# A fused attention and mixture-of-experts kernel: one written list of pieces with named PSUM banks, and means of values put into later blocks by transfers

## The chip, the cores and the metric

The kernel runs on one core of a Trainium2 chip. The metric is the device time of one execution in microseconds (us). One execution of the kernel before was also profiled.

## What is computed

The reference, cut to what matters. `q`, `k`, `v` have the shape (4, 8, 768, 64): batches, heads, positions, head size.

```python
k_sum = k.reshape(B, H, nb, 32, D).max(axis=3)       # nb = 24 blocks of 32 positions
v_sum = v.reshape(B, H, nb, 32, D).mean(axis=3)
scores_l = where(|pos_q - pos_k| < 16, scale * q @ k^T, -1e9)
scores_s = scale * q @ k_sum^T + log(32)
a = softmax(concatenate([scores_l, scores_s]))
x = a @ concatenate([v, v_sum])                      # then (3072 tokens, 512)
e = argmax(x @ w_gate)                               # one of 8 experts for each token
out = softmax(x @ w_gate)[e] * sigmoid(x @ w_output_gate)[e] * (relu(x @ w1[e]) @ w2[e])
```

## The kernel before

Attention goes over 24 tiles of 128 tokens, six to a batch, numbered 0 to 23. A tile is two blocks of 64 queries. A block's keys stand in `kt` (88 columns to a block) and its values in `vw`: 96 rows of neighbouring positions, with rows 64 to 87 kept for the 24 means of the whole batch. One product of a block with `vw` therefore takes in the local window and the summaries. Two copies of `kt` and `vw` alternate by batch.

The steps, with the functions of the code and the tile names that rows of the profile show:

- `load` and `load_vw` (L257) bring `raw_k`, `raw_q` and `vw` from DRAM, mostly from SyncE's queue (SP). `reorder` copies them into `nat_k` and `nat_q` (L246). `prep_k` and `prep_q` transpose them on TensorE (PE) into `ktr` and `qtr` (L291); ACT copies these into `kt` and `qt` (L221), and DVE takes the maximum of keys by block (`km`, L305). `k_sum` spreads it over `kt` (L312).
- `means` (L264, L267) sums values into the bank `ms`; `gather_means` makes `mg` (L273), which ACT copies to `mst`, 24 rows. `put_means` copies `mst` into rows 64 to 87 of the two blocks of a tile, one copy on ACT (L221) and one on DVE (L219).
- `scores` fills `sp` (L333) and DVE adds the mask (`pr`, L338); `smallest` (L345), `subtract` on GpSimd (POOL, L350) and `exps` on ACT (L354) follow. `turn_p` transposes `pr` into `pt` (L365) and ACT copies it to `pT`. `values` multiplies with `vw` into `pv` (L376), and `norm` divides (DVE, L386 to L390) into `xs`. `store_x` writes `xs` to `x_dr` (L395).
- `turn_x` (`xtr`, L402), `logits` (`lp`, L411) and `turn_logits` (`lt`, L419) give the logits of two tiles. `route` finds experts and places for a batch: some eight small DVE operations, the counts `rk` and `tot` on PE (L456 to L461), and six scatters of list entries `l_dr` from POOL (L484).

All PSUM banks of attention come from `bank`, which hands the tags `TR`, `S`, `PT`, `PV`, `S`, `PT`, `PV` round in turn, whatever the piece is.

The experts work in slots of 256 tokens. Slots 0 to 2 take tokens of the first two batches alone, so slot 0 can begin while the attention of the last batch runs. `table` computes the slot table in three steps on DVE. `begin` frees the pool of batches 0 and 2, and issues on SP eight loads `w1l` and four `w2l` for slot 0 (L979) and five `raw` loads for slot 1 (L909), 256 KB each. The first of them needs the expert's number from the slot table. `fetch_list` (`lst`, L866) and `fetch` (`xg`, L881) bring the rows of a slot, `take_plain` transposes them (`xp`, L1007), `early_first` is slot 0's first layer (`hp`, L1017), `early_second` its second (`yp`, L1031). `split` turns a `raw` weight of slot 1 into a high and a low part. From slot 1 on `full` does the same with these parts.

The order of all five engines' queues is the order in which the program is written: attention is recorded under a manual schedule. A loop over tiles i records scores of tile i+2, values of tile i-1, turn_p of i and so on, and dictionaries (`todo`, `put`, `mid`, `rts`, `small`, `scat`) hold what is to be recorded with a later tile. The last tiles and slot 0 are written out by hand behind the loop. A queue works in order, so an instruction that waits holds up all that stands behind it on its engine.

Of the kernel before, what the change touches and what calls it, by code (L numbers as in the profile page):

```python
# [56 lines left out]


# [143 lines left out]
def attention(tc, const, sa, sb, st, ps, dr, q, k, v, id_sb, c_sb, wg_sb, x_dr, l_dr, rt, moe, table, begin, swap):  # L202
# [56 lines left out]
    def means(b, m):  # L259
        if m == 0:  # L260
            mps[b] = ps.tile([P, H * D], F32, name=f"ms{b}", tag="MS", bufs=PB["MS"])
        mp = mps[b]
        for j in range(4):
            nc.tensor.matmul(mp[32 * j:32 * j + 32], lhsT=c_sb[0:LW, C_AVG + 32 * m:C_AVG + 32 * m + 32],  # L264
                             rhs=VW[b % 2][0:LW, 4 * m + j, :, 0:D], start=m == 0, stop=m == 2 and j < 3)
# [17 lines left out]
    ms, km, mps = {}, {}, {}  # L283

    def transposed(kind, b, u, g):
        n = nat[kind, b, u]
# [6 lines left out]
        return pt  # L293

    def prep_k(b, u, g):
        kt = KT[b % 2]
        pt = transposed("k", b, u, g)
        if b not in km:
            km[b] = sb.tile([P, HP, NS], F32, name=f"km{b}", tag="km", bufs=2)
        at = PAD + 4 * u * KW  # L300
        src = pt.rearrange("p x (i s) -> p x i s", s=64)
        dst = kt[:, 2 * g:2 * g + 2, at:at + 4 * KW].rearrange("p x (i w) -> p x i w", w=KW)
        evac(dst[:, :, :, 0:48], src[:, :, :, 0:48])
        evac(dst[:, :, :, 48 + NS:KW], src[:, :, :, 48:64])
        nc.vector.tensor_reduce(out=km[b][:, 2 * g:2 * g + 2, 8 * u:8 * u + 8],  # L305
                                in_=pt.rearrange("p x (n s) -> p x n s", s=32), axis=AX.X, op=ALU.max)
# [16 lines left out]
    def scores(i):  # L323
# [4 lines left out]
        for hp in range(HP):  # L328
            for y in range(2):
                blk = 2 * tok + y  # L330
                for x in range(2):
                    r = slice(64 * x, 64 * x + 64)
                    nc.tensor.matmul(sp[x][64 * y:64 * y + 64, hp, 0:W], lhsT=qt[r, hp, P * tt + 64 * y:P * tt + 64 * y + 64],  # L333
                                     rhs=kt[r, hp, blk * KW:blk * KW + W], start=True, stop=True)
        pr = sb.tile([P, 2, HP, W], F32, name=f"pr{b}{tok}", tag="pr", bufs=BUFS["pr"])
# [20 lines left out]
    def turn_p(i):  # L356
        b, tok = tiles[i]
        pr = prs.pop(i)
        e = i < HELD
        pTs[i] = (sa if e else sb).tile([W, 2, HP, P], F32, name=f"pT{b}{tok}", tag="pTe" if e else "pTl",  # L360
                                        bufs=BUFS["pTe" if e else "pTl"])
        for x in range(2):
            pt = bank([W, HP, P], f"pt{b}{tok}{x}")
            for hp in range(HP):
                nc.tensor.transpose(pt[:, hp, :], pr[:, x, hp, :], id_sb)  # L365
            evac(pTs[i][:, x], pt)

    def values(i):
        b, tok = tiles[i]
        pT = pTs.pop(i)  # L370
        pvs[i] = []
        for g in range(2):
            po = bank([P, 4, D + 1], f"pv{b}{tok}{g}")
            for h in range(4 * g, 4 * g + 4):
                for y in range(2):
                    nc.tensor.matmul(po[64 * y:64 * y + 64, h % 4, :], lhsT=pT[:, h % 2, h // 2, 64 * y:64 * y + 64],  # L376
                                     rhs=VW[b % 2][:, 2 * tok + y, h, 0:D + 1], start=True, stop=True)
            pvs[i].append(po)

    def norm(i):  # L380
# [3 lines left out]
        po = pvs.pop(i)  # L384
# [7 lines left out]
    def store_x(i):  # L392
        b, tok = tiles[i]
        n0 = b * S + tok * P
        (nc.sync if i >= 17 else nc.gpsimd).dma_start(x_dr[n0:n0 + P, :], xss[i].rearrange("p h d -> p (h d)"))  # L395

    def turn_x(i):
        b, tok = tiles[i]
        xs = xss[i]
        xp = bank([P, NC, P], f"xtr{b}{tok}")  # L400
        for c in range(NC):
            nc.tensor.transpose(xp[:, c, :], xs[:, 2 * c:2 * c + 2, :].rearrange("p h d -> p (h d)"), id_sb)  # L402
        if tok % 2 == 0:
            xTs[0] = st.tile([P, NC, 2, P], F32, name=f"xT{b}{tok}", tag="xT", bufs=BUFS["xT"])
        evac(xTs[0][:, :, tok % 2, :], xp)

    def logits(b, tok):

        lp = bank([P, 2 * P], f"lp{b}{tok}")
        for c in range(NC):  # L410
            nc.tensor.matmul(lp[32 * c:32 * c + 32, :], lhsT=wg_sb[:, c, :], rhs=xTs[0][:, c].rearrange("p t n -> p (t n)"),  # L411
                             start=True, stop=True)
        xTs[1] = st.tile([P, 2, P], F32, name=f"ls{b}{tok}", tag="ls", bufs=BUFS["ls"])
        evac(xTs[1].rearrange("p t n -> p (t n)"), lp)

    def turn_logits(b, tok):
        lt = bank([P, 2, 2 * E], f"lt{b}{tok}")
        for t in range(2):
            nc.tensor.matmul(lt[:, t, :], lhsT=xTs[1][:, t, :], rhs=c_sb[:, C_SEL:C_SEL + 2 * E], start=True, stop=True)  # L419
# [6 lines left out]
    def route(b):  # L426
# [29 lines left out]
        nc.tensor.matmul(rk[:, 0:TB, :], lhsT=rt["tri"], rhs=ohb, start=True, stop=False)  # L456
        for sft in range(1, TB):
            nc.tensor.matmul(rk[:, sft:TB, :], lhsT=rt["ones"], rhs=ohb[:, 0:TB - sft, :], start=False, stop=sft == TB - 1)
        tot = bank([P, E], f"tot{b}")
        for t in range(TB):  # L460
            nc.tensor.matmul(tot, lhsT=rt["ones"], rhs=ohb[:, t, :], start=t == 0, stop=t == TB - 1)  # L461
# [55 lines left out]
    for tok in range(2, TB):
        load_vw(0, tok, (0,))
    for g in range(2):
        prep_q(*steps[0], g)  # L520
# [709 lines left out]
```

## Time and profile before

| | us |
|---|---|
| three runs | 533.62, 538.9, 537.9 |
| median | 537.9 |
| profiled execution | 536.84 |
| its span | 535.0 |
| mean granted clock of PE | 0.972 |
| PE busy in the span | 491.0 |

Times in the profile count from the span's start. A row of the timeline gives start, duration, engine, line and tile; the bracket at its end is the idle time of that engine before the row, and what ended it. `SPq` rows are the issues of transfers; how long one travels is given as the time to landing.

### The profile page before, as it was taken

What the parts mean: (1) busy time and instruction counts of PE and PEld (TensorE: products, weight loads), DVE (VectorE), ACT (ScalarE), POOL (GpSimd) and SP (SyncE); (2) the same over time, 40 slices, a digit from 0 to 9 for tenths busy, and PEclk for the clock granted to TensorE, in tenths of its full rate; (3) what the DMA queues carried; (4) which work ended last, traced back from release to release, by engine and by line L of the source; (5) the groups of instructions that cost most, each with busy time, mean ns of one, the idle gap of its engine ahead of it and who ended that gap; (6) DMA issues with size and microseconds to landing.
All of it is one profiled execution on the core that took longest, in us unless ns stands there. A gap on an engine that the chain in (4) does not pass through costs nothing.

```text
span 535.0 us, 12519 instructions
## 1 busy us (share of the span) xinstructions
PE 491.0 (92%) x4348; PEld 405.3 (76%) x4348; DVE 355.1 (66%) x787; ACT 313.1 (59%) x612; POOL 232.8 (44%) x261
## 2 busy tenths in 40 slices
PE   7698999998987799999999999999999989989980
PEld 6556577486666686789898998989899869879870
DVE  3748479679876237797657667665756668668672
ACT  4475677576655545464646655554655567566581
POOL 8737535646684606736433240312224315214221
PEclk9899999998997799999999999999999999999996
DMA  9998957865329328996947748484673966967771
GB/s 235 199 236 199 278 129 179 197 154 128 82 56 324 117 92 266 242 168 193 328 141 254 254 168 312 126 310 150 245 260 137 310 212 216 319 210 228 264 238 29
DMA packets 106114, 109.53 MB, mean 205 GB/s; under 512 B 43150, under 2 KB 67886, under 8 KB 106032
## 3 DMA queue, kind: packets, MB, share of 16 engines
q1 hardware_dynamic: 97216, 90.04, 57.6%
q0 software_dynamic: 8816, 18.51, 11.4%
q8 instruction: 38, 0.62, 0.5%
q14 instruction: 44, 0.36, 0.3%
HBM read 98.33 MB, written 13.59 MB: 209 GB/s over the span
## 4 chain that ended last, share of the span: by engine, by line
PE 69%; ACT 9%; DMA 7%; issue 5%; POOL 4%; DVE 4%; SPq 1%; POOLq 0%; ACTq 0%; DVEq 0%
PE yp L1128 8%; PE yp L1127 8%; PE yp L1126 8%; PE hp L950 8%; PE hp L949 8%; PE hp L948 8%; PE pt L365 3%; PE hp L1017 3%; PE yp L1031 3%; PE pv L376 3%; PE sp L333 2%; ACT pr L354 2%; DMA raw<-in_moe_w_dram 2%; PE xp L930 2%; ACT pT L221 2%
## 5 line engine op out<-in xcount | busy, mean ns | idle before, releaser
L918 DVE TENSOR_TENSOR w2l<-raw,w2h 128x512 fp32r<-128x512 f32 x120 | 79.4, 685 | 40.3 <-ACT w2h L917 38.7
L917 ACT ACTIVATE w2h<-raw 128x512 fp32r<-128x512 f32 x120 | 72.9, 628 | 54.8 <-PE yp L1128 23.7
L950 PE MATMUL hp<-xhl,w1l 128*128 128x256 f32 x352 | 99.4, 283 | 0.0
L949 PE MATMUL hp<-xhl,w1h 128*128 128x256 f32 x352 | 99.4, 283 | 0.0
L948 PE MATMUL hp<-xhl,w1h 128*128 128x256 f32 x352 | 99.4, 284 | 0.0
L881 POOL DMA_INDIRECT xg<-x_dr,lst x34 | 39.3, 1155 | 118.1 <-PE xp L930 110.6
L918 DVE TENSOR_TENSOR w1l<-raw,w1h 128x512 fp32r<-128x512 f32 x117 | 74.5, 687 | 14.8 <-ACT w1h L917 13.5
L1126 PE MATMUL yp<-w2h,hh 128*128 128x512 f32 x200 | 80.1, 400 | 0.0
L1128 PE MATMUL yp<-w2h,hl 128*128 128x512 f32 x200 | 78.7, 394 | 0.1
L1127 PE MATMUL yp<-w2l,hh 128*128 128x512 f32 x200 | 78.6, 393 | 0.0
L917 ACT ACTIVATE w1h<-raw 128x512 fp32r<-128x512 f32 x120 | 67.0, 621 | 8.4 <-DMA raw<-in_moe_w_dram 6.9
L949 PEld LDWEIGHTS hp<-xhl,w1h 128*128 128x128 f32 x352 | 67.4, 191 | 1.1 <-issue 0.2
L948 PEld LDWEIGHTS hp<-xhl,w1h 128*128 128x128 f32 x352 | 67.2, 191 | 1.2 <-issue 0.2
L950 PEld LDWEIGHTS hp<-xhl,w1l 128*128 128x128 f32 x352 | 67.4, 192 | 0.0
L951 ACT ACTIVATE hh<-hp 128x256 fp32r<-128x256 f32 x88 | 33.4, 380 | 52.0 <-PE hp L950 50.4
L350 POOL TENSOR_TENSOR pr<-pr,mn 128x960 f32<-128x960 f32 x24 | 43.1, 1797 | 46.1 <-DVE mn L345 29.1
L952 DVE SCALAR_TENSOR_TENSOR hl<-hp,hh 128x256 fp32r<-128x256 f32 x88 | 35.9, 419 | 35.6 <-ACT hh L951 35.5
L1151 POOL DMA_INDIRECT out_dram<-y,lst x27 | 30.5, 1131 | 55.7 <-DVE y L1148 28.9
L221 ACT ACTIVATE pT<-pt 120x512 f32<-120x512 f32 x48 | 26.8, 596 | 41.2 <-PE pt L365 41.0
L338 DVE TENSOR_TENSOR pr<-sp,c_sb 128x480 f32<-128x480 f32 x48 | 29.2, 649 | 29.2 <-PE sp L333 29.2
L866 POOL DMA_INDIRECT lst<-l_dr,rowib x30 | 31.5, 1051 | 31.9 <-issue 21.8
L1128 PEld LDWEIGHTS yp<-w2h,hl 128*128 128x128 f32 x200 | 37.5, 188 | 8.6 <-DVE hl L1097 0.5
(206 smaller groups left out, 876.9 us busy)
## 6 DMA issues: line engine op xcount, KB each, us to landing
raw<-in_moe_w_dram SPq DMA_DIRECT2D x240, 256.0 KB, 5.2
raw_k<-in_k_dram SPq DMA_DIRECT2D x12, 512.0 KB, 6.0
raw_q<-in_q_dram SPq DMA_DIRECT2D x12, 512.0 KB, 6.2
vw<-in_v_dram SPq DMA_DIRECT2D x44, 128.0 KB, 4.9
x_dr<-xs POOLq DMA_DIRECT2D x17, 256.0 KB, 4.0
vw<-in_v_dram SPq DMA_DIRECT2D x33, 64.0 KB, 5.1
w1l<-in_moe_w_dram SPq DMA_DIRECT2D x8, 256.0 KB, 7.9
w2l<-in_moe_w_dram SPq DMA_DIRECT2D x8, 256.0 KB, 5.7
```

The costliest lines, as they stand in the source:

```text
L221: nc.scalar.activation(dst, src, AF.Copy, scale=1.0 if scale is None else scale)
L350: nc.gpsimd.tensor_tensor(pr, pr, mns.pop(i).unsqueeze(2).to_broadcast([P, H, W]), ALU.subtract)
L881: nc.gpsimd.indirect_dma_start(out=self.xg[t], out_offset=None, in_=self.x_dr[0:rows, :], in_offset=bass.IndirectOffsetOnAxis(ap=self.list ...
L917: nc.scalar.activation(hi, raw, AF.Copy)
L918: (lo_by or nc.vector).tensor_tensor(lo, raw, hi.bitcast(F32), ALU.subtract)
L948: nc.tensor.matmul(hp, lhsT=w_h[:, fs], rhs=self.xh[:, c, :], start=c == 0, stop=False)
L949: nc.tensor.matmul(hp, lhsT=w_h[:, fs], rhs=self.xl[:, c, :], start=False, stop=False)
L950: nc.tensor.matmul(hp, lhsT=w_l[:, fs], rhs=self.xh[:, c, :], start=False, stop=c == NC - 1)
L952: nc.vector.scalar_tensor_tensor(hl[:, j, :], hp, 0.0, hh[:, j, :].bitcast(F32), ALU.max, ALU.subtract)
L1126: nc.tensor.matmul(y, lhsT=hh[:, j, tk], rhs=w_h, start=j == 0, stop=False)
L1127: nc.tensor.matmul(y, lhsT=hh[:, j, tk], rhs=w_l, start=False, stop=False)
L1128: nc.tensor.matmul(y, lhsT=hl[:, j, tk], rhs=w_h, start=False, stop=j == NF - 1)
```

## The change

The loop, the dictionaries and the hand-written end are replaced by one string `ORDER` of 895 words, each a piece, read from left to right. A word is a piece's short name, its arguments, and behind a colon the PSUM banks that it takes. Pieces that write a bank and those that copy it out become words of their own (`pk` and `kk`, `mk`; `tp` and `kp`; `sc` and `ma`; `lg` and `kl`). Every yield of `route` and of the slot table is now one operation, so `route` takes 30 words for a batch (`r`) and the table 26 (`ta`).

A put of means is a word for each block, with the engine that does it: 7 words `pu...a` on ACT, 6 `pu...v` on DVE and 35 `pu...s` as a transfer inside SBUF from SP's queue. The puts of batch 0 are all on ACT and DVE. In slot 0 a `split` is a word too (16 of them, 13 on DVE and 3 on POOL). In slot 1 three steps of the later slot table are taken at a time (`REST`), since each is now one operation.

```diff
+ORDER = """
+lk.0 lk.1 lk.2 lq.0 lq.1 lv.0.0.s lv.1.0.s cl.1 rk.0.v pk.0.0:T kk.0.0 cl.0 mk.0.0 pk.0.1:S kk.0.1 mk.0.1 rk.1.a
...
+r.1 ta ta mi.18 r.1 pu.17.0.s r.1 me.3.1 su.18 st.15.p kp.16.0 kp.16.1 lv.23.0.s lv.23.1.s sc.19:SP ma.19 va.16.0:V
...
-    def put_means(b, tok):
-        for blk in (2 * tok, 2 * tok + 1):
-            evac(VW[b % 2][LW:LW + NS, blk, :, 0:D], ms[b][LW:LW + NS], engine="av"[blk % 2])
+    def put_means(t, y, engine):
+        b, tok = tiles[t]
+        blk = 2 * tok + y
+        if engine == "s":
+            nc.sync.dma_start(VW[b % 2][LW:LW + NS, blk, :, 0:D], ms[b][LW:LW + NS])
+        else:
+            evac(VW[b % 2][LW:LW + NS, blk, :, 0:D], ms[b][LW:LW + NS], engine=engine)
...
     def bank(shape, name):
-        tag = next(turn[0])
+        tag = {"S": "S", "P": "PT", "V": "PV", "T": "TR", "M": "MS"}[banks_of.pop(0)]
         return ps.tile(shape, F32, name=name, tag=tag, bufs=PB[tag])
...
-    for i, (b, tok) in enumerate(tiles[:n - AHEAD]):
...
+    for w in ORDER.split():
+        w, _, at = w.partition(":")
+        banks_of[:] = at
+        name, *args = w.split(".")
+        work[name](*(int(x) if x.isdigit() else x for x in args))
+    return [lambda: route_to(B - 1) for _ in range(TB)]
...
-            made = made or next(rest, None)
+            for _ in range(REST):
+                made = made or next(rest, None)
```

Three places show what this does to the queues. The first is SP's queue at the end of slot 0's and slot 1's first weight loads; `vw` from `mst` is a put, `x_dr` a store of a tile's result. Before:

```order
L909 DMA raw_1_3_2526<-in_moe_w_dram 128x512
L909 ISA
L909 DMA raw_1_4_2528<-in_moe_w_dram 128x512
L395 DMA x_dr<-xs_2569 128x512
L395 DMA x_dr<-xs_2667 128x512
L395 DMA x_dr<-xs_2743 128x512
```

And now:

```order
L845 DMA raw_1_3_2544<-in_moe_w_dram 128x512
L845 ISA
L845 DMA raw_1_4_2546<-in_moe_w_dram 128x512
L344 DMA vw_170<-mst_2349 24x8x64 x2
L462 DMA x_dr<-xs_2569 128x512
L344 DMA vw_170<-mst_2349 24x8x64
L462 DMA x_dr<-xs_2672 128x512
L344 DMA vw_170<-mst_2349 24x8x64 x3
```

The puts of tiles 20 to 23 stand behind all 17 weight loads; before, these puts were copies on ACT and DVE.

The second is DVE's queue at the routing of batch 1 (`mx` to `o` are its small operations, `km` a maximum of keys, `mn` a tile's minimum). Before:

```order
L435 TENSOR_REDUCE mx_1934<-lg_1484 128x6
L437 TENSOR_TENSOR d_1936<-lg_1484,mx_1934 128x48
L439 SCALAR_TENSOR_TENSOR fi_1938<-d_1936,c_sb 128x48
L441 TENSOR_REDUCE first_1940<-fi_1938 128x6
L443 TENSOR_TENSOR oh_1942<-c_sb,first_1940 128x48
L445 CAST ohb_1944<-oh_1942 128x48
L447 TENSOR_TENSOR os_1946<-lg_1484,oh_1942 128x48
L449 TENSOR_REDUCE o_1948<-os_1946 128x6
L345 TENSOR_REDUCE mn_1950<-pr_1890 128x8
L305 TENSOR_REDUCE km_1724<-ktr_1956 128x2x8
L305 TENSOR_REDUCE km_1724<-ktr_1964 128x2x8
```

And now:

```order
L508 TENSOR_REDUCE mx_1926<-lg_1482 128x6
L511 TENSOR_TENSOR d_1928<-lg_1482,mx_1926 128x48
L514 SCALAR_TENSOR_TENSOR fi_1930<-d_1928,c_sb 128x48
L517 TENSOR_REDUCE first_1932<-fi_1930 128x6
L370 TENSOR_REDUCE km_1733<-ktr_1906 128x2x8
L520 TENSOR_TENSOR oh_1936<-c_sb,first_1932 128x48
L686 TENSOR_SCALAR ti_early<-ti_early 128x8
L523 CAST ohb_1945<-oh_1936 128x48
L526 TENSOR_TENSOR os_1962<-lg_1482,oh_1936 128x48
L414 TENSOR_REDUCE mn_1964<-pr_1865 128x8
```

The small operations no longer stand in one block ahead of the minimum and the maxima.

The third is POOL's queue at the start (`nat_k` is the third block of keys, the loads are neighbours of later values). Before:

```order
L215 MEMSET vw_170 24x8x64
L246 COPY nat_k_235<-raw_k_182 128x1024
L257 DMA vw_169<-in_v_dram 32x8x64 x11
L257 DMA vw_169<-in_v_dram 16x8x64
L350 TENSOR_TENSOR pr_317<-pr_317,mn_320 128x960
```

And now:

```order
L271 MEMSET vw_169 24x8x64
L313 DMA vw_169<-in_v_dram 32x8x64 x4
L302 COPY nat_k_239<-raw_k_176 128x1024
L313 DMA vw_169<-in_v_dram 32x8x64 x5
L313 DMA vw_169<-in_v_dram 16x8x64
L313 DMA vw_169<-in_v_dram 32x8x64 x2
L419 TENSOR_TENSOR pr_317<-pr_317,mn_320 128x960
```

Four of the loads moved ahead of the copy. The pieces of `ORDER` on PE between the values of tiles 17 and 20 are, in this order: turn_p 18, turn_x 17, scores 21, values 18, turn_p 19, values 19, query transposes with the logits of tiles 16 and 17, turn_x 18, scores 22, turn_p 20 with turn_logits, turn_x 19, scores 23. Behind values 20 come turn_p 21, logits, values 21, turn_x 20, take_plain, turn_p 22 with turn_logits, and slot 0's first layer.

More of the change, by code (lines that the diff above doesn't have):

```diff
@@ L354, in exps, with turn_p, keep_p, values @@
         nc.scalar.activation(pr, pr, AF.Exp, scale=-1.0)
[L356 removed]
+    def turn_p(i, x):
         b, tok = tiles[i]
[L358 to L368, printed above, removed]
[L369 to L378 removed]
+        pt = banks["pt", i, x] = bank([W, HP, P], f"pt{b}{tok}{x}")
+        for hp in range(HP):
+            nc.tensor.transpose(pt[:, hp, :], prs[i][:, x, hp, :], id_sb)
+    def keep_p(i, x):
+        b, tok = tiles[i]
+        if x == 0:
+            e = i < HELD
+            pTs[i] = (sa if e else sb).tile([W, 2, HP, P], F32, name=f"pT{b}{tok}", tag="pTe" if e else "pTl",
+                                            bufs=BUFS["pTe" if e else "pTl"])
+        evac(pTs[i][:, x], banks.pop(("pt", i, x)))
+    def values(i, g):
+        b, tok = tiles[i]
+        po = banks["pv", i, g] = bank([P, 4, D + 1], f"pv{b}{tok}{g}")
+        for h in range(4 * g, 4 * g + 4):
+            for y in range(2):
+                nc.tensor.matmul(po[64 * y:64 * y + 64, h % 4, :], lhsT=pTs[i][:, h % 2, h // 2, 64 * y:64 * y + 64],
+                                 rhs=VW[b % 2][:, 2 * tok + y, h, 0:D + 1], start=True, stop=True)
     def norm(i):
@@ L383, in norm @@
         den = st.tile([P, H], F32, name=f"den{b}{tok}", tag="den", bufs=BUFS["den"])
-        po = pvs.pop(i)
+        po = [banks.pop(("pv", i, g)) for g in range(2)]
         for g in range(2):
@@ L401, in turn_x, with keep_x @@
         for c in range(NC):
-            nc.tensor.transpose(xp[:, c, :], xs[:, 2 * c:2 * c + 2, :].rearrange("p h d -> p (h d)"), id_sb)
+            nc.tensor.transpose(xp[:, c, :], xss[i][:, 2 * c:2 * c + 2, :].rearrange("p h d -> p (h d)"), id_sb)
+    def keep_x(i):
+        b, tok = tiles[i]
         if tok % 2 == 0:
[L404 to L409, printed above, removed]
+            xTs[i // 2] = st.tile([P, NC, 2, P], F32, name=f"xT{b}{tok}", tag="xT", bufs=BUFS["xT"])
+        evac(xTs[i // 2][:, :, tok % 2, :], banks.pop(("xp", i)))
@@ L517, in attention @@
[L517 to L520, printed above, removed]
-    k_sum(0, "v")
-    for u in range(3):
-        load("k", 1, u)
-    n = len(tiles)
-    live, at, held = {}, {}, []
-    for i in range(n):
-        at[i] = []
-        for _ in range(2):
-            if i > HELD and held:
-                live[held[0]] = i
-                at[i].append(held.pop(0))
-        held.append(i)
-    live[n - 1] = n
-    early, todo, put, scat, rts, end, small, mid = {}, {}, {}, {}, {}, {}, {}, {}
@@ L552, in attention @@
-    for t in range(n):
-        first = live[t - t % TB]
-        later(max(live[t] - 2, first - 1), lambda t=t: put_means(*tiles[t]), put)
-    for i in range(AHEAD):
-        scores(i)
-        smallest(i)
-        subtract(i)
-        if i == 0:
-            reorder("q", *steps[1], "a")
-            load("q", *steps[3])
-            for g in range(2):
-                prep_q(*steps[1], g)
-            exps(0)
-    for i in range(3):
-        later(live[2 * TB - 1] + 4 + i, table, small)
-    plan = {
-        live[2 * TB - 1] + 6: [begin],
-        n - AHEAD - 1: [moe.take_plain],
-    }
@@ L633, in attention @@
-    assert not small and not plan and not pools and not scat and not early and not end
-    b = B - 1
-    def first(j, *n):
-        moe.early_first(j)
-        for x in n:
-            moe.split(1, x)
-    t = n - AHEAD
-    values(t - 1)
-    norm(t - 1)
-    turn_p(t)
-    exps(t + 1)
-    for x in put.pop(t):
-        x()
-    for x in mid.pop(t, []) + rts.pop(t, []):
-        x()
-    assert not todo.pop(t, None) and not put and not todo and not rts and not mid
-    store_x(t - 1)
-    first(0, "v", "p")
@@ L1055, in full_with @@
             if not self.slots.get(EARLY):
-                made = made or next(rest)
+                for _ in range(REST):
+                    made = made or next(rest)
                 if made:
```

365 lines of the change are left out of this document (175 added, 190 removed).

## The prediction

> **What bounds the kernel now.** I read the page first, then busy time by stage, then TensorE's timeline with its gaps, then the DMA-issuing queue of SyncE.
>
> ```profile
> PE 491.0 (92%) x4348; PEld 405.3 (76%) x4348; DVE 355.1 (66%) x787; ACT 313.1 (59%) x612; POOL 232.8 (44%) x261
> ...
> PEclk9899999998997799999999999999999999999996
> ```
>
> TensorE (PE) is the bound; its granted clock dips in the 2nd, 10th, 13th and 14th slice, all in the part that the change rewrites. By stage:
>
> ```profile
> 25.00:151.00 126.00, 116.10 (x1733) 79.78 (x1730) 89.86 (x238) 84.39 (x163) 72.13 (x83) 0.99 0.72 170
> 126.00:133.00 7.00, 4.45 (x48) 3.18 (x43) 6.64 (x21) 3.33 (x8) 4.70 (x8) 0.76 0.79 181
> 151.00:170.80 19.80, 15.66 (x226) 13.03 (x222) 15.57 (x39) 9.48 (x16) 13.45 (x15) 0.83 0.68 204
> 151.00:184.30 33.30, 25.27 (x328) 20.70 (x325) 21.24 (x54) 17.22 (x29) 22.86 (x23) 0.79 0.61 191
> 163.00:170.00 7.00, 7.00 (x88) 6.17 (x84) 5.16 (x10) 1.73 (x4) 4.09 (x5) 0.52 1.02 340
> 177.00:184.00 7.00, 5.74 (x50) 5.00 (x50) 1.59 (x6) 3.95 (x7) 5.35 (x5) 0.52 0.11 36
> 184.30:205.70 21.40, 21.40 (x186) 17.82 (x186) 6.81 (x28) 10.43 (x23) 4.57 (x4) 1.00 0.44 150
> ```
>
> The columns are PE, weight loads, DVE, ACT and POOL busy, granted clock, DMA share and GB/s. From 184.3 us on PE is full at clock 1.00, and nothing that the change moves there makes it shorter. Its prize lies before: 9.9 us idle in 25 to 151 (126.0 - 116.1), 8.0 us in 151 to 184.3 (33.3 - 25.3), and clock halved after the longer gaps. The gaps that matter:
>
> ```profile
> 128.61 0.18 PE L456 MATMUL rk<-ohb,tri 128*128 128x48 bf16 x1 [2.25 <-DVE km L305]
> ...
> 129.20 0.30 PE L461 MATMUL tot<-ohb,ones 128*128 128x8 bf16 x6 [0.30 <-DVE km L305]
> ```
>
> ```profile
> 149.93 1.15 PE L376 MATMUL pv<-vw,pT 120*64 120x65 f32 x32
> ...
> 162.61 1.42 PE L333 MATMUL sp<-kt,qt 64*64 64x120 f32 x32 [2.81 <-ACT qt L221]
> ...
> 170.76 1.15 PE L376 MATMUL pv<-vw,pT 120*64 120x65 f32 x32
> ...
> 177.81 0.48 PE L1007 MATMUL xp<-id_sb,xg 128*128 128x128 f32 x1 [2.82 <-DMA xg<-x_dr,lst]
> ```
>
> The values of tile 17 end at 151.08, those of tile 20 begin at 170.76, and slot 0's first layer begins at 184.3. These are my three landmarks.
>
> **The start: 0.7 us later.** POOL now issues four loads of values ahead of the third block of keys.
>
> ```profile
> 10.68 1.03 POOL L246 COPY nat_k<-raw_k 128x1024 f32<-128x1024 f32 x1
> ...
> 11.66 4.26 POOL L257 DMA_DIRECT2D vw<-in_v_dram  x7
> 11.77 1.09 PE L291 MATMUL ktr<-id_sb,nat_k 128*128 128x128 f32 x8 [0.58 <-POOL nat_k L246]
> ...
> 21.47 1.80 POOL L350 TENSOR_TENSOR pr<-pr,mn 128x960 f32<-128x960 f32 x1
> ...
> 24.36 1.09 PE L365 MATMUL pt<-id_sb,pr 128*120 128x128 f32 x8 [2.38 <-ACT pr L354]
> ```
>
> One issue costs 4.26 / 7 = 0.61 us, so four put the copy, and the key and query transposes behind it, 2.4 us back. About 0.7 us is absorbed, since the first subtraction stood behind POOL's issues anyway, and 1.0 us of means (row below) now fills PE's wait ahead of the first `pt`: 2.4 - 0.7 - 1.0 = 0.7. Bounds 0 and 2.4.
>
> **The middle, 25 to 151: 8.0 us gained.** To win there are 9.9 us of idle time and, at clock 0.76 in 126 to 133, 7.0 x 0.24 = 1.7 us: 11.6 in all. The routing operations, formerly eight in a row on DVE, are now spread, and PE's `rk` comes after other work; I take that gap with its halved clock as gone: 2.25 + 0.3 (the next one) + 1.7 = 4.25. A second class is a bank handed round in turn whose last reader is a late key maximum.
>
> ```profile
> PE pt L365 <- DVE km L305: 1.9, 3, 0.8
> ```
>
> ```profile
> L376 PE MATMUL pv<-vw,pT 120*64 120x65 f32 x768 | 29.4, 233 | 1.4 <-DVE km L305 0.7 <-ACT vw L221 0.6
> ```
>
> With named banks and the maximum apart from the transposes I count these 1.9 and 0.7 as gone: 2.6. Of the remaining 4.75 I take a quarter, 1.15, because the new order shows no reason for more. Sum 8.0; bounds 4.0 and 10.5. What carries ACT and DVE here is slack: 84 and 90 us busy of 126.
>
> **The means of values as transfers.** 35 of the 48 copies into blocks leave ACT and DVE for SP's queue.
>
> ```profile
> L221 ACT ACTIVATE vw<-mst x24: 609/626/628, 37.1 to 185.8; 24x512 f32<-24x512 f32 x24
> L219 DVE COPY vw<-mst x24: 405/419/1844, 37.1 to 183.7; 24x512 f32<-24x512 f32 x24
> ```
>
> That frees 17 x 0.63 = 10.6 us of ACT and 18 x 0.42 = 7.6 of DVE, hidden under PE, hence nothing by itself beyond the gaps counted. But a transfer lands late. No transfer inside SBUF stands in the trace; the nearest are the loads into the same tile:
>
> ```profile
> DMA to landing us min/median/max: 2.9/5.0/9.2
> ```
>
> For batch 1, values of tile 6 come after a copy from PSUM (0.6, as ACT's copies above), two issues (1.2) and a landing of 5.0: 6.8 us. PE has meanwhile, by the chain of waits,
>
> ```profile
> 52.51 1.02 PE pt L365 x8
> 53.53 0.57 PE lp L411 x8
> 54.10 0.99 PE ms L264 x8
> 55.09 1.02 PE xtr L402 x8
> 56.11 0.98 PE sp L333 x32
> 57.09 1.08 PE pv L376 x32
> 58.18 0.55 PE lt L419 x4
> ```
>
> pv 1.08, lt 0.55, pt 1.02, xtr 0.51, eight key transposes 1.02 and sp 0.98: 5.2 us. A wait of 1.7 at the median, none at 2.9; I take 1.0, since a put moves 48 KB, less than those loads. Batch 2 has 7.2 us of such work and waits for nothing at the median. Tile 17's values also get one `lt` (0.55) ahead of them. So they end at 151.1 + 0.7 - 8.0 + 1.0 + 0.55 = **145.3**.
>
> **The queue of SP: the new wait.** Slot 0's weights begin once the slot table is ready, and the trace shows how the queue then behaves:
>
> ```profile
> 152.88 0.35 SPq L395 DMA_DIRECT2D x_dr<-xs  x1
> 155.84 5.42 SPq L979 DMA_DIRECT2D w1l<-in_moe_w_dram  x8
> 162.43 3.33 SPq L979 DMA_DIRECT2D w2l<-in_moe_w_dram  x4
> 166.89 3.16 SPq L909 DMA_DIRECT2D raw<-in_moe_w_dram  x5
> 170.16 26.41 SPq L395 DMA_DIRECT2D x_dr<-xs  x6
> ```
>
> ```profile
> 171.33 2.37 SPq L395 DMA_DIRECT2D x_dr<-xs  x2
> ```
>
> Eight loads go out in 5.4 us, the ninth only 6.6 us after the first; the 18th transfer is issued 14.3 us (170.16) and the 19th 15.5 us (171.33) after the start. A window that opens at 171 gives the last row. Behind them stood stores that nobody awaits. Now the puts of tiles 20 to 23 stand there, and PE's queue is in order: values of tile 20 hold up all behind them.
>
> The weights themselves start 4.8 us after values 17 (155.84 - 151.08); the table's last five operations now follow tile 17's norm without the two copies of 0.42 and the short copy of logits between, 1.0 less: 145.3 + 3.8 = 149.1. The second put of tile 20 is issued 15.5 later and lands 5.0 after that, at 149.1 + 20.5 = 169.6. Bounds of that landing from the same queue, loaded and quiet:
>
> ```profile
> x_dr<-xs SPq DMA_DIRECT2D x2, 256.0 KB, 5.5
> ```
>
> ```profile
> x_dr<-xs SPq DMA_DIRECT2D x1, 256.0 KB, 2.0
> ```
>
> PE's work from values 17 to values 20 is 11.8 us (pt 3.06, xtr 1.53, sp 2.94, pv 2.16, lp 0.57, query transposes 1.02, lt 0.55), so PE is ready at 157.1 and **waits 12.5 us**. Values 20 begin 1.2 us earlier than before, no more.
>
> The Trainium skill, "DMA: Bandwidth & Descriptors", section "Anatomy of one DMA", gives a fixed 2.0 us per transfer and says that the wait for a semaphore sits on the issuing sequencer. The quiet 2.0 us agree, the loaded 5.5 do not; with 2.0 the sum below would come out 3.0 us lower.
>
> **From there to slot 0.** The remaining work is pv 2.16, pt 2.04, lp 0.57, xtr 0.51, lt 0.55 and eight transposes of gathered rows 1.0: 6.8 us, with 0.5 for a copy of `pT` that PE waits for. The wait for gathered rows (2.82) is swallowed by the longer one. After its long idle time PE runs at half clock: the rows at 0.52 last 7 us and cost 3.4; that at 0.76 cost 1.7. I take 3.4. First layer at 169.6 + 6.8 + 0.5 + 3.4 = 180.3 against 184.3: **4.0 us gained**. The work after it is unchanged and PE-bound, so the span is 531.0; with the 1.84 us around it (536.84 - 535.0), **532.8 us**. The median of the runs is 537.9, 1.1 over the profiled execution.
>
> The Trainium skill, "TensorE: Matmul & The Clock Gate", section "Part 1: The HAM clock gate", has one busy window of 3.4 us to recover. By it the loss is 1.7 and the total 531.1; the 7 us rows differ.
>
> Own range: with the low bounds (middle 10.5, start 0, put 0, landing 2.0, clock 1.7) values 17 end at 141.1, values 20 begin at 162.4 and the layer at 171.4, which is 12.9 less: 524. With the high ones (middle 4.0, start 2.4, put 1.7, landing 5.5, clock 3.4) the layer begins at 187.2: 540.
>
> **Rivals.**
> - *The loads drain faster.* At the 340 GB/s of 163 to 170, 17 x 256 KB = 4.46 MB take 13 us and the puts land at 15 after the start: layer at 174.8, total 527.3. For it: nothing else fills the DMA engines then. Against: this rate includes no start-up, and before it took 14.3 us just to issue.
> - *The middle stays as it was.* With 4.0 of 11.6 won, start, put and the longer wait eat it: layer at 184.3, 536.8. For it: 4.75 of the 11.6 have no single cause that the new order takes away. Against: the two classes of 4.25 and 2.6 have one.
> - *The put transfers are slow (the other side).* At a landing of 8 us values 6 wait 4.7, values 12 wait 2.7, each with 1.7 of halved clock, and values 20 begin 23.5 after the weights: the middle loses 4.05, weights start at 158.9, layer at 193.1, total 545.6. It turns the whole to a loss from about 6 us, and to one over 1% from about 7.2. For it: landings reach 9.2 us. Against: the median of 5.0.
> - That the change doesn't do what it says is out: the built order shows 35 puts on SP, those of tiles 20 to 23 behind the weights.
>
> **How the numbers follow.** Mine 0.44, faster drain 0.22, unchanged middle 0.16, slow puts 0.18. A change of 1% (5.4 us) is about what a measurement of this kernel tells from none. Of mine, 0.19 lie beyond it on the fast side, 0.23 within, 0.02 on the slow side. Faster 0.19 + 0.22 = 0.41; same 0.23 + 0.16 = 0.39; slower 0.02 + 0.18 = 0.20. The range 521 to 542 holds my case, most of the faster drain and the milder slow puts.
>
> **What would show it.** Right: PE's gap ahead of `rk` gone; the values of tile 20 preceded by the longest gap of the attention (8 to 14 us), released by a put; its landing 19 to 22 us after the first weight load; values 17 ending near 145. Wrong: a gap there under 5 us (faster), or gaps over 3 us ahead of the values of tiles 6 and 12 (slow puts).

## The result, and the profile after

The changed kernel takes 562.85 us (median of four runs), the kernel before 538.4 in the same measurement: 1.046 times as long, 95% interval 1.038 to 1.054. The forecast was 532.8, with 521 to 542 as its range, so it missed by 30 us and on the wrong side. Some executions fall into a slower state; medians in this document are over all of them and ratios over the others alone, against the kernel before on the same chip, so a ratio need not be the quotient of two medians.

The page of the changed kernel, its lines on TensorE:

```profile
span 561.5 us, 13020 instructions
...
PE 512.4 (91%) x4500; PEld 426.3 (76%) x4500; DVE 359.8 (64%) x796; ACT 314.8 (56%) x622; POOL 240.9 (43%) x267
```

TensorE's idle time in the span grew by 5.1 us (561.5 - 512.4 = 49.1 against 535.0 - 491.0 = 44.0), its busy time by 21.4 us, with 4500 matmuls against 4348. Waits do not add matmuls; more work was done. The next two fences are the view of groups, of before and of after (count behind the x, then busy us and mean ns):

```profile
L948 PE MATMUL hp<-xhl,w1h 128*128 128x256 f32 x352 | 99.4, 284 | 0.0
L1126 PE MATMUL yp<-w2h,hh 128*128 128x512 f32 x200 | 80.1, 400 | 0.0
```

```profile
L884 PE MATMUL hp<-xhl,w1h 128*128 128x256 f32 x384 | 108.5, 284 | 1.2 <-ACT w2h L853 1.2
L1067 PE MATMUL yp<-w2h,hh 128*128 128x512 f32 x216 | 86.4, 400 | 0.0
```

A full slot issues 32 of the first rows (8 hidden blocks by 4 parts) and 16 of the second (8 by 2). 384 - 352 = 32 and 216 - 200 = 16: after runs exactly **one full slot more**, 12 for 11, each matmul at the old price.

Where the span went, by three landmarks in the traces: slot 0's first layer begins at 189.5 us (184.3 before); the last matmul ends at 551.4 (522.4 before); the span ends at 561.5 (535.0). So +5.2 us up to the first layer, +23.8 in the experts (361.8 against 338.0), -2.5 in the tail behind the last matmul (10.2 against 12.7; the last slot is now a full one, before it was a half one). Sum 26.5, the whole difference of the spans.

TensorE's timeline of after, with the gaps of attention:

```profile
46.01 1.14 PE L444 MATMUL pv<-vw,pT 120*64 120x65 f32 x16 [2.40 <-DVE km L370]
...
129.94 1.15 PE L444 MATMUL pv<-vw,pT 120*64 120x65 f32 x32 [1.54 <-DMA vw<-mst]
131.02 0.20 PE L538 MATMUL rk<-ohb,tri 128*128 128x48 bf16 x1
...
150.70 1.79 PE L323 MATMUL ms<-vw,c_sb 120*32 120x512 f32 x2 [2.93 <-DMA vw<-in_v_dram]
...
181.14 2.00 PE L444 MATMUL pv<-vw,pT 120*64 120x65 f32 x32 [7.60 <-DMA vw<-mst]
...
189.54 0.81 PE L952 MATMUL hp<-xhl,w1l 128*128 128x256 f32 x3
```

`rk` has no gap any more. The longest gap of attention stands ahead of the values of tile 20 and is ended by a put (`vw` from `mst`). New are the gaps ahead of the values of tiles 1 (2.40), 14 (1.54), 15 (1.26) and 18 (1.15) and of the sums of batch 3 (2.93). Values of tile 17 end at 157.9 us (151.1 before). SP's queue, which the long gap waits for:

```profile
161.35 5.28 SPq L915 DMA_DIRECT2D w1l<-in_moe_w_dram  x8
166.82 2.17 SPq L915 DMA_DIRECT2D w2l<-in_moe_w_dram  x4
169.81 3.96 SPq L845 DMA_DIRECT2D raw<-in_moe_w_dram  x5
173.82 1.75 SPq L344 DMA_DIRECT2D vw<-mst  x2
```

**Where the slot comes from.** The slot table's first operation, `ti_early`, reads `base`, the running count of tokens by expert, which every batch's routing adds to. DVE's timeline at that place, before and then after:

```profile
131.66 0.16 DVE L464 TENSOR_TENSOR base<-base,tot 128x8 f32<-128x8 f32 x1
139.88 0.17 DVE L753 TENSOR_TENSOR ti_early<-base,c_sb 128x8 int32<-128x8 f32 x1
```

```profile
121.32 0.15 DVE L684 TENSOR_TENSOR ti_early<-base,c_sb 128x8 int32<-128x8 f32 x1
127.44 0.34 DVE L686 TENSOR_SCALAR ti_early<-ti_early 128x8 int32<-128x8 int32 x1
132.73 0.16 DVE L549 TENSOR_TENSOR base<-base,tot 128x8 f32<-128x8 f32 x1
```

Before, batch 1's counts are added 8.2 us ahead of the read. After, the read comes 11.4 us ahead of the addition: the word `ta` stands among the words `r.1`, and only the 14th `r.1` adds. So the table of slots 0 to 2 is made from batch 0 alone. Counting the reference's inputs by expert, batch 0 has 172 and 596 tokens for two experts, which gives 596 // 256 = 2 full slots; batch 1 gives a third expert 768, three more. With both batches there are tokens for all three early slots; with batch 0 alone, slot 2 stays empty. It costs its full time none the less (its first layer begins at 249.1 us, the next slot's at 272.6, 23.5 us later), and its 256 tokens take a slot at the end. Every token is still computed, since the later table starts from what the early one took.

### The profile page after: what moved, and what is told of

It is laid out like the page before. It is cut to its first block, busy times and chain, and to the rows that moved or that the text cites. A ratio compares the mean times of both kernels' runs of the same rounds, so it can differ in the third digit from the quotient of the medians.

```text
span 561.5 us, 13020 instructions
## 1 busy us (share of the span) xinstructions
PE 512.4 (91%) x4500; PEld 426.3 (76%) x4500; DVE 359.8 (64%) x796; ACT 314.8 (56%) x622; POOL 240.9 (43%) x267
## 3 DMA queue, kind: packets, MB, share of 16 engines
q0 software_dynamic: 9200, 18.72, 10.7%
## 5 line engine op out<-in xcount | busy, mean ns | idle before, releaser
L854 DVE TENSOR_TENSOR w2l<-raw,w2h 128x512 fp32r<-128x512 f32 x128 | 85.0, 687 | 44.2 <-ACT w2h L853 41.6
L884 PE MATMUL hp<-xhl,w1h 128*128 128x256 f32 x384 | 108.5, 284 | 1.2 <-ACT w2h L853 1.2
L886 PE MATMUL hp<-xhl,w1l 128*128 128x256 f32 x384 | 108.5, 283 | 0.0
L885 PE MATMUL hp<-xhl,w1h 128*128 128x256 f32 x384 | 108.5, 283 | 0.0
L817 POOL DMA_INDIRECT xg<-x_dr,lst x36 | 43.2, 1200 | 129.3 <-PE xp L866 110.4
L854 DVE TENSOR_TENSOR w1l<-raw,w1h 128x512 fp32r<-128x512 f32 x125 | 79.8, 688 | 14.7 <-ACT w1h L853 13.1
L1067 PE MATMUL yp<-w2h,hh 128*128 128x512 f32 x216 | 86.4, 400 | 0.0
L1068 PE MATMUL yp<-w2l,hh 128*128 128x512 f32 x216 | 85.0, 393 | 0.0
L1069 PE MATMUL yp<-w2h,hl 128*128 128x512 f32 x216 | 84.9, 394 | 0.0
L884 PEld LDWEIGHTS hp<-xhl,w1h 128*128 128x128 f32 x384 | 73.4, 191 | 2.8 <-ACT w2h L853 1.6
L885 PEld LDWEIGHTS hp<-xhl,w1h 128*128 128x128 f32 x384 | 73.5, 191 | 1.2 <-issue 0.2
L886 PEld LDWEIGHTS hp<-xhl,w1l 128*128 128x128 f32 x384 | 73.6, 192 | 0.0
L1067 PEld LDWEIGHTS yp<-w2h,hh 128*128 128x128 f32 x216 | 40.7, 188 | 8.1
```

The source lines that it names most:

```text
L817: nc.gpsimd.indirect_dma_start(out=self.xg[t], out_offset=None, in_=self.x_dr[0:rows, :], in_offset=bass.IndirectOffsetOnAxis(ap=self.list ...
L854: (lo_by or nc.vector).tensor_tensor(lo, raw, hi.bitcast(F32), ALU.subtract)
L884: nc.tensor.matmul(hp, lhsT=w_h[:, fs], rhs=self.xh[:, c, :], start=c == 0, stop=False)
L885: nc.tensor.matmul(hp, lhsT=w_h[:, fs], rhs=self.xl[:, c, :], start=False, stop=False)
L886: nc.tensor.matmul(hp, lhsT=w_l[:, fs], rhs=self.xh[:, c, :], start=False, stop=c == NC - 1)
L1067: nc.tensor.matmul(y, lhsT=hh[:, j, tk], rhs=w_h, start=j == 0, stop=False)
```

## The experiments

Ratios are to the kernel before on the same chip. E1 to E4 ran on one chip, E5 to E7 on a second, E8 and E9 on a third; the kernel before took 537.4, 536.2 and 536.3 us there.

| | median us | ratio | 95% interval |
|---|---|---|---|
| after | 562.85 | 1.046 | 1.038 to 1.054 |
| E1 table behind the counts | 539.01 | 1.004 | 1.001 to 1.008 |
| E2 before, table from batch 0 | 559.13 | 1.039 | 1.032 to 1.046 |
| E3 E1, puts of tiles 20 to 23 on ACT and DVE | 532.76 | 0.984 | 0.973 to 0.996 |
| E4 E1, all puts on ACT and DVE | 530.53 | 0.984 | 0.976 to 0.992 |
| E7 E1, puts of tiles 20 to 23 ahead of the weights | 532.02 | 0.993 | 0.989 to 0.997 |
| E5 E4, two banks renamed | 527.94 | 0.985 | 0.980 to 0.990 |
| E6 E5, two copies of the start earlier | 526.38 | 0.983 | 0.980 to 0.987 |
| E8 E6, first puts away from POOL's work | 527.66 | 0.982 | 0.978 to 0.987 |
| E9 E8, last puts earlier | 524.96 | 0.980 | 0.977 to 0.984 |

Theory: the loss is the additional slot. Rival: it is the waits of attention, puts and SP's queue above all.

**E1, the table behind the counts.**

```diff
-... kq.8.1 ta pk.10.0:P kk.10.0 ...
+... kq.8.1 pk.10.0:P kk.10.0 ...
-... tp.14.1:T ta r.1 rq.9.p ...
+... tp.14.1:T r.1 rq.9.p ...
-r.1 r.1 r.1:S r.1:P r.1 r.1 tp.15.0:V ...
+r.1 r.1 r.1:S r.1:P r.1 r.1 ta ta tp.15.0:V ...
```

> The changed kernel, but the first two operations of the early slot table (L684, L686) stand behind batch 1's update of the token counts (L549) again. Theory (the table was made from batch 0's counts alone, so one of the three early slots had no tokens and one full slot more had to run later): rows of L884 fall from 384 to 352, TensorE busy from 512 to about 491, the last matmul comes 23.5 us earlier (the spacing of the slots), and the time falls from 562.9 to 538 to 542. Rival (the loss is all in the waits of attention: puts and the queue of SP, with the later work merely shifted): the time stays above 555, and the rows of L884 stay at 384.

539.0 us, 23.8 less than after. Groups and timeline of E1:

```profile
L884 PE MATMUL hp<-xhl,w1h 128*128 128x256 f32 x352 | 99.4, 284 | 0.0
```

```profile
178.60 2.00 PE L444 MATMUL pv<-vw,pT 120*64 120x65 f32 x32 [7.72 <-DMA vw<-mst]
...
186.91 1.89 PE L952 MATMUL hp<-xhl,w1l 128*128 128x256 f32 x8
```

The 32 rows are gone, and the wait of 7.7 us ahead of tile 20 is still there: two words of a list of 895, moved, took the loss away. Without it the changed kernel takes 0.4% longer than the one before (0.1 to 0.8%), less than the 1% that the prediction calls a difference.

**E2, the same fault put into the kernel before.**

```diff
         nc.vector.tensor_tensor(rt["base"], rt["base"], tot, ALU.add)
+        if b == 0:
+            rt["base0"] = st.tile([P, E], F32, name="base0", tag="base0", bufs=1)
+            nc.vector.tensor_copy(rt["base0"], rt["base"])
...
-    nc.vector.tensor_tensor(ti, rt["base"], base, ALU.subtract)
+    nc.vector.tensor_tensor(ti, rt["base0"], base, ALU.subtract)
```

> The kernel before with one thing changed: the early slot table reads a copy of the counts taken after batch 0, instead of the counts of batches 0 and 1. The order of attention, banks and puts are those of before; one small DVE copy is added. Theory: 352 rows of L948 become 384, one full slot of 23.5 us is added at the end, less some 2.5 us of a shorter tail since a full slot and not a half one comes last: 558 to 562. Rival (the early table costs nothing by itself): 537 to 540.

```profile
L951 PE MATMUL hp<-xhl,w1h 128*128 128x256 f32 x384 | 108.6, 284 | 2.8 <-issue 2.8
```

559.1 us, 21.7 above before's 537.4, with the 384 rows. The rival falls from both sides: with the old attention the slot costs nearly what after lost, and the new attention without it loses under 1%.

**E3, E4 and E7: the puts.** E3 writes `pu.20.1.v` for `pu.20.1.s` and so on for the eight puts of tiles 20 to 23, E4 for all 35, E7 leaves the eight as transfers and moves their words:

```diff
-be va.18.0:T ma.21 ... tp.19.1:V pu.20.1.s kp.19.1 ex.20 pu.20.0.s ...
+pu.20.1.s pu.20.0.s pu.21.1.s pu.21.0.s pu.22.1.s pu.22.0.s pu.23.0.s pu.23.1.s be va.18.0:T ma.21 ...
```

> E1's kernel with the eight puts of tiles 20 to 23 as copies on ACT and DVE in place of transfers on SP's queue behind the weight loads. Theory (my prediction's step on SP's queue): the wait of 7.6 us ahead of the values of tile 20 goes, and the 1.9 us of halved clock behind it; slot 0's first layer comes 4 to 9.5 us earlier than in E1 (189.5), and the time is 4 to 9 us below E1's. Rival (rows gathered for slot 0, or its weights, come at the same time anyway): another wait takes its place ahead of slot 0's first layer, and the time is within 2 us of E1's.

> E1's kernel with all 35 puts as copies on ACT (even blocks) and DVE (odd blocks) and none on SP's queue. Theory (SP's issues of puts at some 0.83 us each delay both the puts and the later loads of values): besides the 7.6 us, the waits ahead of values (1.54, 1.26, 1.15) and the 2.93 ahead of the sums of batch 3 go as well, and values of tile 17 begin 4 to 7 us earlier than in E1; the time is 3 to 6 us below E3's, 528 to 534. Rival (ACT and DVE become the bound with 35 more copies of 0.63 and 0.42): waits for ACT and DVE take their place, and the time is not below E3's.

> E1's kernel, in which the puts of tiles 20 to 23 stay transfers on SP's queue, but stand ahead of the 17 weight loads and not behind them. Theory (their place behind the loads is what costs, as the prediction's step on SP's queue had it): the wait of 7.7 us ahead of the values of tile 20 goes; the weights start up to 6.6 us later (eight issues of 0.83) without TensorE waiting for them long, and the time is 3 to 7 us below E1's 539.0, near E3's 532.8. Rival (the transfers themselves are what costs, or the later weights hold up slot 0's first layer): within 2 us of E1's or above.

E3 and then E7, TensorE's timeline:

```profile
169.30 1.15 PE L444 MATMUL pv<-vw,pT 120*64 120x65 f32 x32
...
172.93 1.15 PE L444 MATMUL pv<-vw,pT 120*64 120x65 f32 x32 [0.88 <-ACT vw L277]
...
177.98 0.81 PE L942 MATMUL xp<-id_sb,xg 128*128 128x128 f32 x3 [2.82 <-DMA xg<-x_dr,lst]
...
181.71 1.89 PE L952 MATMUL hp<-xhl,w1l 128*128 128x256 f32 x8
```

```profile
129.82 2.00 PE L444 MATMUL pv<-vw,pT 120*64 120x65 f32 x32 [5.26 <-DMA vw<-mst]
...
170.52 1.15 PE L444 MATMUL pv<-vw,pT 120*64 120x65 f32 x32
...
177.31 1.89 PE L952 MATMUL hp<-xhl,w1l 128*128 128x256 f32 x8
```

In both the wait ahead of tile 20 is gone (no bracket at 169.30 and 170.52). E3 gives 2.8 of the 7.7 us back to the wait for gathered rows, as its rival had it in part, and still wins 6 us. E7 shows that the place in the queue is what costs, not that the puts are transfers: the weights start at 165.7, 9 us later than in E1, and TensorE does not wait for them.

```profile
118.51 0.85 SPq L344 DMA_DIRECT2D vw<-mst  x1
...
155.39 8.89 SPq L344 DMA_DIRECT2D vw<-mst  x8
165.70 5.91 SPq L915 DMA_DIRECT2D w1l<-in_moe_w_dram  x8
```

The later weights are not free, though. Slot 0's first layer begins 9.6 us earlier than in E1 (177.31 for 186.91), but the span is only 5.3 us shorter (531.2 for 536.5): 4.3 us are lost behind that point. The stores of `xs` stand behind the 17 loads, SP issues them from 178.8 us, and DVE has to wait for one before it can write `xs` again; TensorE waits in turn for `xs`, and its granted clock is 0.92 from 177.3 to 200.0, where E3 has 1.00 in the same work (181.7 to 204.4). E7's DVE and TensorE:

```profile
184.98 0.76 DVE L457 TENSOR_TENSOR xs<-pv,den 128x256 f32<-128x256 f32 x2 [4.25 <-DMA x_dr<-xs]
```

```profile
185.46 0.88 PE L468 MATMUL xtr<-id_sb,xs 128*128 128x128 f32 x4 [2.42 <-DVE xs L457]
```

E4 against E3 was to be 3 to 6 us; the ratios are the same (0.984 both), and E3's interval alone is over 2% wide, so the times don't tell the two apart. The traces do: the gaps ended by puts are gone in E4, other gaps came, and values of tile 17 begin at 151.7 for 151.9 in E3, not 4 to 7 us earlier. The stage up to tile 17 is as long as before. Busy time from the first values of tile 0 to those of tile 17 shows it: E1, then E4 (columns as before, window's length in front of TensorE's busy time):

```profile
41.30:152.20 110.90, 102.50 (x1552) 74.61 (x1546) 77.60 (x218) 67.19 (x137) 65.65 (x78) 0.97 0.79 171
```

```profile
41.30:151.70 110.40, 101.30 (x1550) 73.34 (x1546) 84.08 (x229) 76.63 (x151) 65.88 (x77) 0.98 0.72 162
```

And the same stage of the kernel before:

```profile
38.30:149.90 111.60, 102.64 (x1546) 71.92 (x1540) 83.57 (x228) 75.07 (x148) 65.01 (x77) 0.98 0.70 166
```

Idle: 9.0 us before, 8.4 in E1, 9.1 in E4. E2, which has the old order, takes 110.4 us for this stage. The new order wins nothing there, with puts as transfers or without.

**E5, two banks.** `va.1.1:S` becomes `va.1.1:M` and `va.6.0:P` becomes `va.6.0:M`, so that neither stands on a bank whose last reader is a late key maximum.

> E4's kernel with two banks renamed: the second half of the values of tile 1 and the first half of those of tile 6 go into the bank MS, which is free there, instead of banks whose last reader is a late key maximum (waits of 2.40 and 1.73 us in E4, both ended by L370). Theory (the middle of attention won nothing since the named banks bring the waits for key maxima back at other places): both waits and the halved clock behind the first go, values of tile 17 begin 3 to 6 us earlier than in E4 (151.7), and the time falls from 530.5 to 525 to 528. Rival (the middle is held by many small waits that take up whatever is won): values of tile 17 begin within 1.5 us of E4's, and the time is the same within 1.5 us.

```profile
46.91 1.80 PE L429 MATMUL pt<-id_sb,pr 128*120 128x128 f32 x8 [2.53 <-DVE km L370]
...
82.57 1.06 PE L356 MATMUL qtr<-id_sb,nat_q 128*128 128x128 f32 x8 [1.98 <-DVE xs L457]
```

The theory fell. The two waits moved on to the next pieces, 2.40 into 2.53 and 1.73 into 1.98, and values of tile 17 begin at 151.6 for 151.7. The time of 527.9 lies in the 525 to 528 that the theory gave, but the ratio is E4's (0.985 for 0.984), so that tells nothing. The bank was only where a late DVE was noticed.

**E8, what makes DVE late.** E4's DVE and POOL at 40 us, where `km` is awaited:

```profile
40.05 4.88 DVE L275 COPY vw<-mst 24x512 f32<-24x512 f32 x4 [2.85 <-ACT mst L277]
44.96 1.29 DVE L370 TENSOR_REDUCE km<-ktr 128x16 f32<-128x512 f32 x2
```

```profile
39.32 1.04 POOL L302 COPY nat_q<-raw_q 128x1024 f32<-128x1024 f32 x1 [4.39 <-DMA raw_q<-in_q_dram]
40.33 1.96 POOL L419 TENSOR_TENSOR pr<-pr,mn 128x960 f32<-128x960 f32 x1
42.24 2.41 POOL L302 COPY nat_k<-raw_k 128x1024 f32<-128x1024 f32 x2
```

And the same four copies in the kernel before, at a time when POOL had nothing to do:

```profile
37.06 1.42 DVE L219 COPY vw<-mst 24x512 f32<-24x512 f32 x4 [4.04 <-ACT mst L221]
```

Four copies of 0.42 us took 4.9 beside POOL's work. E8 (on top of E6, below) takes them away from there:

```diff
-... pu.0.0.a pu.0.1.v pu.1.0.a pu.1.1.v pu.3.0.a pu.2.1.v pu.3.1.v rq.3.p pk.3.0:S pu.2.0.a kk.3.0 ...
+... pu.0.0.a pu.0.1.a pu.1.0.a pu.1.1.a rq.3.p pk.3.0:S kk.3.0 ...
-... va.1.1:M no.1 tp.3.0:P ...
+... va.1.1:M no.1 pu.2.0.a pu.2.1.v pu.3.0.a pu.3.1.v tp.3.0:P ...
```

> E6's kernel with the first eight puts of batch 0 taken from under GpSimd's work: those of tiles 0 and 1 on ACT alone, those of tiles 2 and 3 (two on ACT, two on DVE) behind the norm of tile 1, when GpSimd is idle. Theory (a DVE copy into vw takes 0.42 us alone, but lasts as long as GpSimd's work beside it: four of them took 4.3 to 4.9 us at 40 us, next to GpSimd's subtraction and copies, and the key maxima behind them came late): no DVE copy of a put takes over 1 us before 60 us, the wait for L370 ahead of tile 3's transposes (1.69 us in E6) shrinks to under 0.5, and values of tile 2 begin 1.5 to 2.5 us earlier, counted from values 0. Rival (DVE is late there for another reason, as its copies only wait for ACT's mst): the wait stays over 1.2. For the time I expect 524 to 526 by the theory, if the later waits don't take the gain up; 526.4 if they do.

```profile
43.07 1.29 DVE L370 TENSOR_REDUCE km<-ktr 128x16 f32<-128x512 f32 x2 [5.75 <-ACT kt L277]
...
47.85 0.75 DVE L275 COPY vw<-mst 24x512 f32<-24x512 f32 x2
```

```profile
44.42 1.22 PE L429 MATMUL pt<-id_sb,pr 128*120 128x128 f32 x8 [0.86 <-DVE km L370]
```

Two copies take 0.75 us now, the maxima start 1.8 us sooner than in E6 (44.8), and the wait is 0.86 for 1.69, more than the 0.5 expected. From values 0 to values 2 it takes 8.5 us for 10.7. Values of tile 17 begin 108.2 us after values 0 (109.6 in E6): the one edit to the middle that shortened it by more than 1 us. E8 takes the copies away whole, so it shows that they held the maxima up; that it was their slowing, and not their own 1.7 us, is read from the rows above. The time itself is not below E6's. In its profiled execution slot 0 waits 3.0 us for gathered rows, and the granted clock is 0.94 in 150 to 180 us, where E6 had 1.00.

**E6, the start.** `rk.2.p` goes ahead of `pk.1.0:P` and thus of POOL's loads, `rq.0.v` ahead of `pk.2.0:T` and thus of the last key maxima.

> E5's kernel with two copies of the start earlier in their queues: POOL's copy of the third block of keys ahead of its loads of values, and DVE's copy of the first block of queries ahead of the last two key maxima. Theory (TensorE waits 2.1 us for each of the two, and then runs at half clock): both waits shrink to under 1 us, values of tile 0 begin 2 to 4 us earlier than in E5, and the time is 2 to 4 us below E5's. Rival (the clock's halved stretch at the start comes whatever the waits are, as the kernel before showed it too): at most 1 us.

E5 and then E6, in two windows of the start:

```profile
8.00:28.00 20.00, 12.43 (x145) 9.61 (x144) 10.45 (x19) 8.94 (x20) 12.22 (x20) 0.74 1.22 221
28.00:45.00 17.00, 13.73 (x215) 8.67 (x213) 11.26 (x13) 11.60 (x21) 12.36 (x9) 1.00 1.06 205
```

```profile
8.00:28.00 20.00, 13.28 (x185) 8.90 (x184) 14.04 (x24) 10.75 (x23) 14.20 (x22) 1.00 1.24 220
28.00:45.00 17.00, 15.13 (x176) 8.91 (x173) 7.82 (x9) 9.66 (x18) 10.50 (x8) 0.80 1.11 212
```

The rival holds. The two waits shrink (2.85 and 2.07 in E5 to 0.58 and 0.58), but the halved clock only moves from the first window (0.74) to the second (0.80), and values of tile 0 begin at 41.7 for 42.0. E2, which has the start of the kernel before, began them at 41.6, the kernel before itself at 38.3: executions differ by more than this term.

**E9, the last puts earlier.** The eight copies of E4's kind for tiles 20 to 23 go behind the norms of tiles 18 and 19 (`no.18 pu.20.1.v pu.20.0.a pu.21.1.v pu.21.0.a`, and so on).

> E8's kernel with the puts of tiles 20 to 23 earlier in ACT's and DVE's queues (behind the norms of tiles 18 and 19). Theory: the wait of 0.87 us for the put ahead of the values of tile 21 goes, slot 0's first layer begins up to 0.9 us earlier than in E8; the time is E8's less 0 to 1 us. Rival (rows gathered for slot 0 are what slot 0 waits for, so the gain goes into the wait ahead of L942): first layer and time as in E8 within 0.3 us of the trace.

```profile
170.19 0.33 PE L942 MATMUL xp<-id_sb,xg 128*128 128x128 f32 x1 [1.25 <-DMA xg<-x_dr,lst]
171.75 0.55 PE L942 MATMUL xp<-id_sb,xg 128*128 128x128 f32 x3 [1.24 <-DMA xg<-x_dr,lst]
```

The wait of 0.87 ahead of tile 21 is gone; 2.5 us of wait for gathered rows stand behind it. From values of tile 17 to slot 0's first layer E9 takes 25.7 us, E8 28.3 and E6 25.5: the gain went into that wait, as the rival had it, and E8 was the late one. 525.0 us is the lowest of all, 0.980 of before (0.977 to 0.984), so E9 beats both kernels. Its interval and E8's overlap, and what E9 is below E8 is more than the 0 to 1 us expected, so the last step is not shown to be worth anything.

## Why the prediction was wrong, step by step

- **"The work after it is unchanged and PE-bound."** This is the step that failed. It was PE-bound, and not unchanged: 23.8 us more, of 30 missed. I followed the moved table only as something that is ready sooner, and priced its operations, but not what it reads. The rows were in hand: in the order of DVE's queue that the section on the change shows, L686 `ti_early` stands among the first operations of batch 1's routing, while the counts are added near that routing's end. "That the change doesn't do what it says is out" was said of the puts alone. E1 and E2 show the cause from both sides.
- **The middle, 8.0 us.** E1 shows it without the slot: from values 0 to values 17 it is 0.7 us shorter (110.9 for 111.6), where the forecast had 8.0 less 1.55 for the puts and one `lt`. In after it is 4.1 us longer (115.7), with the wait of 2.93 for loads of values in it. The gap ahead of `rk` is gone, as forecast. But 2.6 us of waits for key maxima, which I counted as gone "with named banks", came back at another place (2.40 ahead of tile 1), because the order bunches four copies on DVE next to POOL's work. E5 shows that the banks were not the cause, E8 that the copies were, for about half of what was left of that wait (1.69 to 0.86). The rest is a string of small gaps; it takes up what is won at one place, and I did not settle why its sum stays at 8 to 9 us.
- **The puts' landing, 5.0 us.** The put for tile 14 is issued at 118.51 in E7 and its values begin at 129.82: 11.3 us, and 6.4 for the second put of tile 20 in after (174.77 to 181.14, where the row at 173.82 issues two). The wait ahead of tile 14 was 1.54 in after, 2.59 in E1, 4.62 in E3 and 5.26 in E7. Ahead of tiles 6 and 12, where the rival of slow puts looked for waits over 3 us, after has none for a put. The section of the Trainium skill that the prediction names for a fixed 2.0 us ("DMA: Bandwidth & Descriptors", "Anatomy of one DMA") is on transfers issued from GpSimd; the puts go by SP. The row of the loads was the nearest that I had, and its upper end, 9.2, was nearer the truth than its median. In after the last loads of values are issued by 145.5 us, 9 us later than before, with puts of 0.83 us an issue among them, and the sums of batch 3 wait 2.93 us for one; in E1's profile, by 143.3, they did not wait.
- **The queue of SP.** The mechanism was right. The put landed 181.14 - 161.35 = 19.8 us after the first weight load (forecast 20.5, sign 19 to 22). That it came so near is partly luck: it was issued 13.4 us behind that load and not 15.5, and took 6.4 us and not 5.0. The wait was 7.6, under the forecast 12.5 and just under its sign of 8, since TensorE itself came to that place 12.2 us after the first weight load (173.54), not 8.0. E3 and E7 took the wait away, and the time fell by some 6 us (E7: 0.993 for 1.004). The stores behind the loads, which "nobody awaits", were awaited once the loads came 9 us later (E7).
- **The halved clock behind it, 3.4 us.** Mis-sized: from 181.14 the values and transposes take 2.00 and some 1.9 us for 1.15 and 1.09, 1.7 us in all. The Trainium skill, "TensorE: Matmul & The Clock Gate", section "Part 1: The HAM clock gate", has one busy window of 3.4 us, which the prediction set aside. The trace agrees with it here: the slow rows end 3.8 us after the restart (181.14 to 184.97). The 7 us at 163 to 170 of the kernel before don't agree, with TensorE busy all through; what decides between the two is open.
- **The start, 0.7 us.** POOL's copy came 1.87 us later (12.55 for 10.68) and values of tile 0 began 2.8 us later, but E2 with the old start was as late. The term can't be told from the scatter of executions.
- **Slot 0's first layer at 180.3.** 189.5 in after, 186.9 in E1. The rival of an unchanged middle described the change without the slot best: its 536.8 stands beside E1's 539.0. No rival had a change in the work of the experts.

## What to carry to other kernels

When a piece is moved in a written order, check what it reads before what it costs: find the last write ahead of it that should count, and ask whether the program's control depends on the value. An earlier read can leave the output as it was and change how much work is run; the counts of the groups behind it show this at once, before any wait is looked at. A transfer put into a queue costs what stands ahead of it in that queue, so a short one that somebody waits for goes ahead of long ones that nobody awaits yet (E7: some 6 us for eight moved words, after the later stores had taken a part back).

## What the runs showed of the hardware

- A DVE copy of 24x512 f32 inside SBUF takes 0.42 us while POOL is idle, and up to 2.0 us while POOL works: the four copies in the rows of E4 took 0.60, 2.00, 1.25 and 1.25, each ending some 0.3 us behind one of POOL's operations. POOL's own operations lost less (1.96 for 1.79, 2.41 for 2.02). The Trainium skill, "SBUF — State Buffer", section "SBUF: two separate sides", says that GpSimd and some kinds of DVE operations share a pair of ports as an exclusive lock, so that the loser is held for a whole instruction. The rows agree for DVE as the loser.
- A put of 48 KB is about 204 packets under 512 bytes (50290 such packets in E1, 43150 in E4, for 35 puts), and its issue takes SP 0.83 us (0.6 for a load of values). Around 120 us, where the put for tile 14 was under way, E1's DMA engines were at a share of 1.41 for 135 GB/s, those of E4, without puts, at 0.49 for 128:

```profile
120.00:125.00 5.00, 4.53 (x85) 3.76 (x84) 4.03 (x9) 4.12 (x9) 4.81 (x7) 1.00 1.41 135
```

```profile
120.00:125.00 5.00, 4.83 (x88) 3.96 (x84) 4.66 (x14) 4.27 (x9) 4.65 (x9) 1.00 0.49 128
```

The loads of values are not at the same times in the two, so how much of it is the puts' own is not shown.
